# Forgetting attention with a channel mix on one core: the softmax division moved from the weights to the finished output

## The chip, the cores and the metric

The kernel runs on one core of a Trainium2 chip. Its time is device microseconds from the first to the last instruction of one execution; three runs of the kernel before took 919.32, 919.80 and 922.17 us, so 919.8 us is its median. A separate execution was taken by the hardware profiler, and everything said of instructions below comes from that one.

The core has five engines with a queue of instructions each: PE multiplies matrices, DVE, ACT and POOL work elementwise on vectors, and SP here issues every DMA. An engine takes its instructions strictly in the order in which the program lists them, so an instruction that waits also holds what stands behind it in its queue.

## The reference

```python
def _attn_ref(q, k, v, s):                    # 8 batches, 8 heads, 576 positions, head size 64
    scores = np.matmul(q, k.transpose(0, 1, 3, 2)) / np.sqrt(D)
    cum = np.cumsum(np.maximum(s, 0.0), axis=-1)
    bias = -(cum[:, :, :, None] - cum[:, :, None, :])
    scores = np.where(causal, -1e9, scores + np.minimum(bias, 0.0))
    attn = np.exp(scores - np.max(scores, axis=-1, keepdims=True))
    attn = attn / (np.sum(attn, axis=-1, keepdims=True) + 1e-09)
    return np.matmul(attn, v)

def _moe_ref(x, mu_k, mu_r, w_k, w_v, w_r):   # x: the 8 heads side by side, 512 wide; d_ff 1024
    x_prev = x shifted by one position, zero at the first
    xk = mu_k * x + (1.0 - mu_k) * x_prev
    xr = mu_r * x + (1.0 - mu_r) * x_prev
    k = np.maximum(xk @ w_k, 0.0)
    return 1.0 / (1.0 + np.exp(-(xr @ w_r))) * (k * k @ w_v)
```

The weights `w_k`, `w_v`, `w_r` arrive in double precision.

## The kernel before

**Attention, one head at a time.** A visit is one pair of heads of one batch. The 576 queries are cut into five tiles `t`: 64 queries first, then four times 128. Tile `t` sees keys 0 to `KN[t]` = 64, 192, 320, 448 or 576. Batch 0 is visited twice per pair, first with the tiles 0 to 2 (called A) and, when all four pairs are through, with the tiles 3 and 4 (called Z), so that the first rows of its output are ready early; the batches 1 to 7 are visited once per pair with all five tiles. That makes 4 + 4 + 28 = 36 visits and 72 heads' turns.

In `scores` a head's turn goes like this. PE multiplies queries by keys (L678; operands are split in a high and a low part, `KH` and `KL`, `G` holds both parts of q). DVE adds the bias `cb` or the masked bias `mask` and keeps the running minimum (L693), writing into the tile `W`. ACT takes the exponential of a whole row of tiles in place, with the row's sum in `sums` (L711). When all tiles of the head are through, POOL adds 1e-9 to the sums (L748), DVE takes the reciprocal `rinv` (L753), and POOL multiplies each tile of `W` by its row's reciprocal (L724): a query lies on a partition here, so the reciprocal is one scalar per partition. Rows 0 to 63 of tile 0 fill only 64 partitions.

`weighted` then turns `W` by PE transposes (L770; keys now lie on partitions), ACT and DVE split each turned block in a high part `ph` and a low part `pl` (L797, L801, L829, L836), PE multiplies by the values `V` (L903), and ACT and DVE add the two halves of the product into `xT` (L933, L937). `xT` holds the output of the pair transposed: partition 64 j + d is component d of head j, a column is a query. `finish` calls `weighted` for head j one head later than `scores`, and after the second head SP writes `xT` to the DRAM tensor `x_d` (L1231).

**Preparation.** POOL also makes the low parts of k, q and v (`KL` L607, `G` L618, `V` L563), the masks (L649) and the low parts of the weights (L538), which DVE and ACT first put together from the halves of the double precision words (L507 to L536).

**Channel mix.** 18 chunks of 256 positions. Each loads `x` from `x_d` (L1132), mixes it with its shifted self (ACT L979, DVE L988), splits the result (L1007, L1011), and then runs `hidden` (L1040), `gate` (L1082) and `output` (L1107) on PE. There is one buffer `x`, so the load for the next chunk waits until the last mix of the chunk before has read it.

**What sets the order.** All operations are first collected as tasks in a `Plan`. A task has an engine, an assumed duration, its dependencies and a due time, set by the program for each visit and chunk (`plan.due`). `Plan.forward` deals the tasks out engine by engine, earliest due time first among those that are ready, with assumed durations and assumed gaps between engines; `Plan.backward` derives new due times from the result; eight rounds are made, and the order of the best is emitted. So a change in a task's engine or length can move instructions everywhere in the program. While PE has nothing to do at the start, the plan fills it with multiplications of the identity (L359).

Of the kernel before, what the change touches and what calls it, by code (L numbers as in the profile page):

```python
# [285 lines left out]
def forgetting_attention_then_channel_mix(  # L286
# [19 lines left out]
    P = 128  # L306
# [18 lines left out]
    def sbuf(shape, tag, bufs=1, dtype=F32):  # L325
        return plan.buffer(sb, shape, dtype, tag, bufs)
# [4 lines left out]
    def fixed(t):  # L331
        b = Buffer(lambda: t)
        b.ap = t
        return b
# [13 lines left out]
    def pool(emit, reads, writes, n, extra, rate=0.8333):  # L348
        return plan.add("POOL", n * rate + extra, emit, reads, writes)

    def dma(emit, reads, writes, ns):
        return plan.add("SP", max(520, ns), emit, reads, writes, land=1300)
# [272 lines left out]
    def scores(b, h, tiles, G, KH, KL):  # L625
# [93 lines left out]
                [(nm, (t, mi))], [(W, i) for i in range(3)] + [(sums, t)], n, 280, 1,  # L719
            )  # L720

        def normalize(t, m, n, W):
            pool(
                lambda: nc.gpsimd.tensor_scalar(  # L724
                    out=W.ap[:m, :n],
                    in0=W.ap[:m, :n],
                    scalar1=rinv.get()[:m, t : t + 1],
                    scalar2=1.0,
                    op0=ALU.mult,
                    op1=ALU.mult,  # L730
                ),
                [rinv], [(W, i) for i in range(3)], n, 244,
            )

        def rs(x):
            return x.get()[:, tiles[0] : tiles[-1] + 1]

# [13 lines left out]
            [(sums, t) for t in tiles], [rinv], len(tiles), 100,  # L751
        )
        dve(lambda: nc.vector.reciprocal(rs(rinv), rs(rinv)), [], [rinv], 8 * len(tiles))  # L753
        for t in tiles:
            normalize(t, QN[t], KN[t], pt[t])
        return pt

    def weighted(j, pt, V, xT, tiles, plain):
# [194 lines left out]

    x_d = [fixed(dram.tile([P, NP, S + 1], F32, name=f"x_d{b}")) for b in range(B)]

    def channel_mix(ch, start, span):
# [263 lines left out]
    def finish(j, pt, V, xT, n, due):  # L1222
        b, hp, tiles = visits[n]
        plan.due = due
        weighted(j, pt, V, xT, tiles, n < PLAIN)
        if j == 1:
            q0, q1 = QS[tiles[0]], QS[tiles[-1]] + QN[tiles[-1]]

            c = slice(1 + q0 if q0 else 0, 1 + q1)
            dma(  # L1230
                lambda: nc.sync.dma_start(x_d[b].ap[:, hp, c], xT.get()[:, c]),  # L1231
                [(xT, 2)] + [(xT, (i, x)) for i in range(2) for x, _ in sums_of(tiles)],
                [(x_d[b], (hp, y)) for y in range(2) if tiles is ALL or y == (q0 > 0)],
                819,
            )
            if hp == NP - 1:
                there[b] = q1
# [69 lines left out]
```

## Time and profile before

| | us |
|---|---|
| median of three runs | 919.8 |
| span of the profiled execution | 919.5 |
| PE busy | 872.8 |
| DVE busy | 696.3 |
| ACT busy | 693.1 |
| POOL busy | 519.1 |
| of it, L724 (the division) | 165.2 |

The page gives busy time as a union over one engine; matrix multiplications overlap one another, so a PE that is always busy can still be short of its peak. The clock that PE was granted (1.00 is full speed) is given per stretch of time. "A <- B" in a table of waits means that A stood idle until B let it go. DMA issues are listed under SPq, the queue of SP; the time from issue to landing is given beside them.

### The profile page before, as it was taken

Reading aid. Unit: us, or ns where it says so; the run is one execution under the profiler, and the core shown is the slowest. Engines: PE = TensorE matmul, PEld = TensorE weight load, DVE = VectorE, ACT = ScalarE, POOL = GpSimd, SP = SyncE. Lnnn points to the kernel's source line nnn. Section 1 sums busy time; section 2 is a strip of 40 time slices with the busy share of each in tenths; the row PEclk is TensorE's granted clock in tenths of the full one; section 3 lists DMA queues with packets and bytes.
Section 4 is the critical chain, followed back from the end, with each engine's and each line's share of the span. In section 5 each row is a group of like instructions: output and inputs, shape, how many; then the busy total and the mean of one; then the engine's idle time right before and its main releaser. Section 6 shows DMA issues by size and latency. Waiting matters only on the chain. (4 is left out here: it accounts for less than half of the span.)

```text
span 919.5 us, 18649 instructions
## 1 busy us (share of the span) xinstructions
PE 872.8 (95%) x5546; PEld 758.6 (83%) x5546; DVE 696.3 (76%) x2473; ACT 693.1 (75%) x1834; POOL 519.1 (56%) x884
## 2 busy tenths in 40 slices
PE   6877879999999999999999999999999999998998
PEld 4656858987988898988889898989898979887886
DVE  6897998987987788778878778777787887546431
ACT  5888888998997898788968787878787876445331
POOL 6999599898576566556665646565556461100000
PEclk7568989999999999999999999999999999999999
DMA  6798645645344343434353525252434230101100
GB/s 195 223 257 237 206 123 160 174 142 168 100 151 129 109 152 87 145 112 144 100 151 93 163 61 159 79 152 79 147 97 138 79 89 25 42 31 35 46 24 23
DMA packets 65045, 110.89 MB, mean 121 GB/s; under 512 B 10544, under 2 KB 26416, under 8 KB 64944
## 3 DMA queue, kind: packets, MB, share of 16 engines
q1 hardware_dynamic: 64944, 109.71, 40.2%
q8 instruction: 43, 0.70, 0.3%
q14 instruction: 58, 0.48, 0.2%
HBM read 90.64 MB, written 19.04 MB: 119 GB/s over the span
## 5 line engine op out<-in xcount | busy, mean ns | idle before, releaser
L1040 PE MATMUL m<-xh,w_k 128*128 128x256 f32 x1152 | 231.4, 287 | 4.4 <-DVE kl L1069 4.4
L711 ACT ACTIVATE W<-W,nm 64x64 f32<-64x64 f32 (+4 forms) x320 | 179.7, 562 | 41.3 <-DVE nm L693 36.7
L770 PE MATMUL t<-ident,W 128*128 128x128 f32 (+1 forms) x960 | 188.3, 284 | 16.6 <-DVE ph L844 4.8
L1107 PE MATMUL m<-w_v,kh 128*128 128x512 f32 x576 | 198.4, 403 | 0.0
L1040 PEld LDWEIGHTS m<-xh,w_k 128*128 128x128 f32 x1152 | 186.2, 190 | 6.2 <-DVE kl L1069 4.8
L724 POOL TENSOR_SCALAR W<-W,rinv 64x64 f32<-64x64 f32 (+4 forms) x320 | 165.2, 538 | 10.6 <-DVE rinv L753 6.1
L1040 PE MATMUL m<-xl,w_k 128*128 128x256 f32 x576 | 164.6, 286 | 0.0
L770 PEld LDWEIGHTS t<-ident,W 128*128 128x128 f32 (+1 forms) x960 | 114.3, 133 | 47.5 <-DVE pl L801 7.9
L607 POOL TENSOR_TENSOR KL<-raw,KH 128x576 fp32r<-128x576 f32 (+1 forms) x72 | 98.5, 1370 | 79.8 <-ACT KH L603 73.4
L678 PE MATMUL s<-KH,G 128*128 128x288 f32 (+4 forms) x384 | 125.3, 335 | 11.3 <-ACT KH L603 5.3
L801 DVE TENSOR_TENSOR pl<-t,ph 128x256 fp32r<-128x256 f32 (+3 forms) x264 | 122.2, 472 | 16.0 <-ACT ph L797 14.7
L1107 PEld LDWEIGHTS m<-w_v,kh 128*128 128x128 f32 x576 | 106.2, 189 | 18.2 <-DVE r L530 0.2
L678 PE MATMUL s<-KL,G 128*128 128x288 f32 (+4 forms) x384 | 118.5, 312 | 2.4 <-POOL KL L607 2.4
L797 ACT CAST ph<-t 128x256 fp32r<-128x256 f32 (+3 forms) x264 | 107.3, 414 | 13.0 <-PE t L770 11.5
L1107 PE MATMUL m<-w_v,kl 128*128 128x512 f32 x288 | 117.0, 406 | 0.0
L693 DVE CUSTOM_DVE_ANT_0 W<-s,cb 128x320 f32<-128x320 f32 (+3 forms) x256 | 94.9, 375 | 26.4 <-PE s L678 21.7
L903 PE MATMUL po<-ph,V 128*128 128x448 f32 (+4 forms) x344 | 109.6, 326 | 3.7 <-ACT ph L797 1.8
L1040 PEld LDWEIGHTS m<-xl,w_k 128*128 128x128 f32 x576 | 109.2, 190 | 0.9
L618 POOL TENSOR_TENSOR G<-raw,G 64x576 fp32r<-64x576 f32 (+2 forms) x72 | 93.6, 1300 | 27.4 <-issue 13.2
L988 DVE SCALAR_TENSOR_TENSOR xp<-x,mu,xp 128x256 f32<-128x256 f32 (+3 forms) x192 | 80.4, 419 | 37.2 <-ACT xp L979 33.9
L979 ACT ACTIVATE xp<-x,mu 128x256 f32<-128x256 f32 (+3 forms) x192 | 81.5, 424 | 29.3 <-DVE xl L1011 9.7
L1082 PE MATMUL m<-w_r,xh 128*128 128x512 f32 x288 | 101.9, 407 | 0.0
(97 smaller groups left out, 1751.7 us busy)
## 6 DMA issues: line engine op xcount, KB each, us to landing
raw<-in_k SPq DMA_DIRECT2D x128, 144.0 KB, 3.2
cb<-cum_d SPq DMA_DIRECT2D x64, 288.0 KB, 3.6
raw<-in_q SPq DMA_DIRECT2D x112, 144.0 KB, 3.3
vn<-in_v SPq DMA_DIRECT2D x32, 320.0 KB, 3.8
out<-g SPq DMA_DIRECT2D x36, 256.0 KB, 2.1
x_d<-xT SPq DMA_DIRECT2D x28, 288.5 KB, 2.3
x<-x_d SPq DMA_DIRECT2D x12, 514.0 KB, 4.0
w_k<-in_moe_w_k SPq DMA_DIRECT2D x8, 512.0 KB, 5.3
```

Of the source, the lines that this page charges most:

```text
L607: lambda k=k, kh=kh, kl=kl: nc.gpsimd.tensor_tensor(out=kl.get(), in0=k.get(), in1=f32(kh.get()), op=ALU.subtract),
L678: lambda x=x, K=K: nc.tensor.matmul(ps.get()[:m, :w], G.get()[:, q0 : q0 + m], K.get()[:, k0 : k0 + w], start=x == 0, stop=x == 1,),
L693: lambda a=a, e=e, bias=bias, i=i: nc.vector.tensor_tensor_reduce(out=W.ap[:m, a:e], in0=ps.get()[:m, a - k0 : e - k0], in1=bias.get()[:m, ...
L711: lambda: nc.scalar.activation(W.ap[:m, :n], W.ap[:m, :n], AF.Exp, bias=nm.get()[:m, 3 * t + mi : 3 * t + mi + 1], scale=-1.0, accum_out=s ...
L724: lambda: nc.gpsimd.tensor_scalar(out=W.ap[:m, :n], in0=W.ap[:m, :n], scalar1=rinv.get()[:m, t : t + 1], scalar2=1.0, op0=ALU.mult, op1=AL ...
L770: lambda: nc.tensor.transpose(ps.get()[0:m, place : place + P], pt[t].ap[:, k0 : k0 + m], ident.ap),
L797: act(lambda: nc.scalar.copy(strips(ph), src()), [ps], [(ph, k) for k in ks], n * m)
L801: lambda: nc.vector.tensor_tensor(out=strips(pl), in0=src(), in1=f32(strips(ph)), op=ALU.subtract),
L903: lambda: nc.tensor.matmul(po.get()[: P if both else 64, at + q0 - base : at + q0 - base + m], V.get()[:, kb, 2 * j : 2 * j + (2 if both e ...
L1040: lambda u=u, f=f, c=c, n=n, w=w, x=x: nc.tensor.matmul(ps.get()[:, u * CT : (u + 1) * CT], weight["k", c, f // 4].get()[:, w, f % 4 * P : ...
L1082: lambda c=c, n=n, x=x, w=w: nc.tensor.matmul(ps.get(), x.get()[:, c, ts], weight["r", c, 0].get()[:, w], start=c == 0 and n == 0, stop=c ...
L1107: lambda f=f, n=n, x=x, w=w: nc.tensor.matmul(ps.get(), x.get()[:, f, ts], weight["v", f, 0].get()[:, w], start=f == 0 and n == 0, stop=f ...
```

## The change

The tiles `W` stay as the exponentials leave them. `normalize` is removed. Instead, each head's reciprocals go by DMA to a new DRAM tensor `rinv_d` of the batch, laid out by head and query: tile 0 (64 partitions, one column) in one DMA, the other tiles (128 partitions, one column each) in a second, so that each element of 4 bytes lands on its own. When the second head of a pair is finished, two DMAs read the rows of both heads back, each broadcast to 64 partitions, into a new tile `R` with two buffers, so that `R` has the layout of `xT`. POOL multiplies the finished `xT` by `R` once, and only then SP writes `xT` to `x_d`. The last line of the diff shrinks a reserve of on-chip memory that belongs to DMAs issued by POOL, of which the kernel has none.

```diff
-        def normalize(t, m, n, W):
-            pool(
-                lambda: nc.gpsimd.tensor_scalar(
-                    out=W.ap[:m, :n],
-                    in0=W.ap[:m, :n],
-                    scalar1=rinv.get()[:m, t : t + 1],
-                    scalar2=1.0,
-                    op0=ALU.mult,
-                    op1=ALU.mult,
-                ),
-                [rinv], [(W, i) for i in range(3)], n, 244,
-            )
-
 ...
         dve(lambda: nc.vector.reciprocal(rs(rinv), rs(rinv)), [], [rinv], 8 * len(tiles))
-        for t in tiles:
-            normalize(t, QN[t], KN[t], pt[t])
+        for ts in ((0,), tuple(t for t in tiles if t)):
+            if ts[0] in tiles:
+                q0, m, n = QS[ts[0]], QN[ts[0]], len(ts)
+                dma(
+                    lambda ts=ts, q0=q0, m=m, n=n: nc.sync.dma_start(
+                        rinv_d[b].ap[h, q0 : q0 + n * m].rearrange("(t p) -> p t", p=m),
+                        rinv.get()[:m, ts[0] : ts[-1] + 1],
+                    ),
+                    [rinv], [(rinv_d[b], (h, t)) for t in ts], 100 * n,
+                )
         return pt
 ...
+    rinv_d = [fixed(dram.tile([H, S], F32, name=f"rinv_d{b}")) for b in range(B)]
     x_d = [fixed(dram.tile([P, NP, S + 1], F32, name=f"x_d{b}")) for b in range(B)]
 ...
         if j == 1:
             q0, q1 = QS[tiles[0]], QS[tiles[-1]] + QN[tiles[-1]]
 
+            R = sbuf([P, q1 - q0], "R", 2)
+            for i in range(2):
+                dma(
+                    lambda i=i: nc.sync.dma_start(
+                        R.get()[64 * i : 64 * i + 64],
+                        rinv_d[b].ap[2 * hp + i : 2 * hp + i + 1, q0:q1].broadcast_to([64, q1 - q0]),
+                    ),
+                    [(rinv_d[b], (2 * hp + i, t)) for t in tiles], [(R, i)], 410 * (q1 - q0) / S,
+                )
+            parts = [(xT, (i, x)) for i in range(2) for x, _ in sums_of(tiles)]
+            pool(
+                lambda: nc.gpsimd.tensor_tensor(
+                    out=xT.get()[:, 1 + q0 : 1 + q1],
+                    in0=xT.get()[:, 1 + q0 : 1 + q1],
+                    in1=R.get(),
+                    op=ALU.mult,
+                ),
+                [(R, 0), (R, 1)], parts, q1 - q0, 114, 2.21,
+            )
             c = slice(1 + q0 if q0 else 0, 1 + q1)
             dma(
                 lambda: nc.sync.dma_start(x_d[b].ap[:, hp, c], xT.get()[:, c]),
 ...
-    nc = bacc.Bacc("TRN2", target_bir_lowering=False, num_devices=1)
+    nc = bacc.Bacc("TRN2", target_bir_lowering=False, num_devices=1, dynamic_dma_scratch_size=1024)
```

The numbers 100, 410, 114 and 2.21 are what the plan assumes of the new tasks; they set its order, not their true length.

**How the order moves.** The first pairs of batch 0 on POOL. `rinv_293` and `rinv_338` are the reciprocals of the two heads of the first pair, `W_0_...` and `W_1_...` their weight tiles; `KL`, `G`, `V` and `mask` are prepared for heads to come. Before:

```order
L724 TENSOR_SCALAR W_0_72<-W_0_72,rinv_293 128x192
L724 TENSOR_SCALAR W_0_73<-W_0_73,rinv_293 128x320
L748 TENSOR_SCALAR rinv_338<-sums_115 128x3
L607 TENSOR_TENSOR KL_340<-raw_101,KH_312 128x320
L607 TENSOR_TENSOR KL_219<-raw_106,KH_214 128x320
L724 TENSOR_SCALAR W_1_76<-W_1_76,rinv_338 64x64
L649 AFFINE_SELECT mask_183<-cb_155 64x64
L724 TENSOR_SCALAR W_1_77<-W_1_77,rinv_338 128x192
L649 AFFINE_SELECT mask_183<-cb_155 128x256
L724 TENSOR_SCALAR W_1_78<-W_1_78,rinv_338 128x320
```

After, the same place (line numbers are the changed kernel's):

```order
L618 TENSOR_TENSOR G_189<-raw_109,G_189 64x320
L563 TENSOR_TENSOR V_312<-vn_161,V_312 128x3x64
L607 TENSOR_TENSOR KL_336<-raw_111,KH_326 128x320
L735 TENSOR_SCALAR rinv_347<-sums_120 128x3
L563 TENSOR_TENSOR V_312<-vn_161,V_312 128x3x64
L607 TENSOR_TENSOR KL_251<-raw_114,KH_230 128x320
L618 TENSOR_TENSOR G_217<-raw_149,G_217 64x320
L637 MEMSET sums_120 128x1
L538 TENSOR_TENSOR w_k_00_362<-xh_215,w_k_00_362 128x512
L607 TENSOR_TENSOR KL_261<-raw_111,KH_244 128x320
```

The divisions are gone and the preparation of the next pairs follows directly on the reciprocal.

SP's queue up to the first write of `x_d`. `raw` are k and q on their way to be split, `cb` the bias rows, `w_k` a block of the weights. Before:

```order
L630 DMA cb_168<-cum_d 128x320
L588 DMA raw_101<-in_k 64x320 x2
L588 DMA raw_103<-in_q 64x320
L588 DMA raw_106<-in_k 64x320 x2
L588 DMA raw_103<-in_q 64x320
L484 DMA w_k_10_526<-in_moe_w_k 128x1024
L630 DMA cb_155<-cum_d 128x320
L1231 DMA x_d_89<-xT_110 128x321
```

After:

```order
L1228 DMA R_445<-rinv_d_89 64x320
L630 DMA cb_178<-cum_d 128x320
L1228 DMA R_445<-rinv_d_89 64x320
L484 DMA w_k_10_460<-in_moe_w_k 128x1024
L588 DMA raw_114<-in_k 64x320
L588 DMA raw_109<-in_q 64x320
L745 DMA rinv_d_89<-rinv_307 64x1
L745 DMA rinv_d_89<-rinv_307 128x2x1
L588 DMA raw_109<-in_q 64x320
L630 DMA cb_178<-cum_d 128x320
L588 DMA raw_114<-in_k 64x320
L1246 DMA x_d_97<-xT_134 128x321
```

Two reads of `R` and two writes of reciprocals now stand between the loads of k, q and `cb`; the write of a head's reciprocals comes several rows ahead of the read of the same values.

SP's queue at the end of the attention: the last two pairs, and the load of `x` for the third chunk from the end, whose first columns come from batch 6 and whose last 65 wait for the last pair of batch 7. Before:

```order
L1231 DMA x_d_96<-xT_110 128x577
L1132 DMA x_918<-x_d_95 128x4x193
L1124 DMA out<-g_1306 128x512
L1124 DMA out<-g_1375 128x512
L1231 DMA x_d_96<-xT_128 128x577
L1132 DMA x_918<-x_d_96 128x4x65
```

After:

```order
L1228 DMA R_539<-rinv_d_96 64x576
L1246 DMA x_d_104<-xT_134 128x577
L745 DMA rinv_d_96<-rinv_347 64x1
L745 DMA rinv_d_96<-rinv_347 128x4x1
L1128 DMA x_895<-x_d_103 128x4x193
L1228 DMA R_539<-rinv_d_96 64x576
L1120 DMA out<-g_1291 128x512
L1120 DMA out<-g_1357 128x512
L1246 DMA x_d_104<-xT_138 128x577
L1128 DMA x_895<-x_d_104 128x4x65
```

Both halves of the last `R` are read ahead of two writes of `out`, so before the last `x_d`; the last `x_d` now waits for POOL's product instead of DVE's sum.

## The prediction, made before the change was run

> **What bounds the kernel now.** I read the stretches first, since the share of busy time over the whole span mixes three very different parts.
>
> ```profile
> core 0: us, PE busy (x) PEld busy (x) DVE busy (x) ACT busy (x) POOL busy (x), PEclk, DMA share, GB/s
> 0.00:20.00 20.00, 12.01 (x61) 8.56 (x62) 11.20 (x32) 10.61 (x25) 13.07 (x38) 0.80 0.71 196
> 20.00:67.00 47.00, 37.95 (x161) 27.35 (x160) 43.26 (x161) 38.43 (x121) 43.44 (x86) 0.61 0.80 236
> 67.00:92.00 25.00, 19.29 (x111) 15.35 (x110) 19.98 (x62) 20.91 (x51) 23.53 (x31) 0.80 0.86 237
> 92.00:141.00 49.00, 39.76 (x232) 33.21 (x232) 47.16 (x158) 42.11 (x104) 38.00 (x55) 0.90 0.52 164
> 184.00:736.00 552.00, 544.99 (x3625) 482.66 (x3625) 439.88 (x1659) 455.12 (x1229) 342.07 (x579) 1.00 0.41 122
> 812.00:842.00 30.00, 27.51 (x167) 24.19 (x165) 14.80 (x30) 13.36 (x29) 0.00 (x0) 1.00 0.15 50
> ```
>
> From 184 to 736 us PE is busy 544.99 of 552.00 us at full clock: there PE is the bound, and an engine that becomes less busy beside it earns almost nothing. After 812 us POOL is empty. What a lighter POOL can earn lies in batch 0, from 20 to 92 us: POOL is busy 43.44 of 47.00 and 23.53 of 25.00 us, 93% of 72 us. But DVE is at 43.26 of 47.00 beside it, and from 92 to 141 us DVE is the fullest engine with 47.16 of 49.00 us, or 96.2%. The DMAs are at 0.80 and 0.86. PE is not the bound there.
>
> Next, who waited for the division, and for what PE waits from 20 to 67 us:
>
> ```profile
> engine op xcount: duration ns min/median/max, first and last start us, forms
> ...
>   PEld t L770: 6.7, 13
>   PE t L770: 3.0, 6
> ```
> ```profile
> PEld po L903 <- ACT ph L797: 4.7, 8, 1.1
> PEld t L770 <- DVE pl L836: 4.2, 7, 1.5
> ...
> PEld t L770 <- POOL W L724: 3.2, 6, 1.0
> ...
> PE t L770 <- POOL W L724: 1.4, 3, 0.8
> ```
>
> The first two rows are the waiters on L724 over the whole span: PE lost 3.0 us in 6 waits, its weight loads 6.7 us. In the front ACT and DVE hold up PE's loads at least as long (4.7 and 4.2 us) as POOL's division does (3.2 us).
>
> **What is removed.** POOL's 320 divisions, by stretch:
>
> ```profile
> 20.00:67.00 47.00, 11.26 (x26) 0.61 0.80 236
> 67.00:141.00 74.00, 12.20 (x19) 0.86 0.64 189
> 141.00:812.00 671.00, 141.74 (x275) 1.00 0.39 117
> sum 792.00, POOL 165.20; mean POOL 55.07
> ```
> ```profile
> 67.00:92.00 25.00, 4.12 (x6) 0.80 0.86 237
> ```
> ```profile
> L724 POOL TENSOR_SCALAR W<-W,rinv 64x64 f32<-64x64 f32 (+4 forms) x26 | 11.3, 445 | 0.1
> ```
>
> From 20 to 92 us that is 11.26 + 4.12 = 15.4 us of POOL's 67.0. The last row is the group from 20 to 67 us: only 0.1 us of idle time stood before its 26 instructions, so POOL was never waiting for them to become ready; they were late because POOL was full.
>
> **What POOL gets instead.** 36 products of two inputs on `xT`. The trace has the same operation and shape as KL and, for the 256 columns of a Z visit, as G:
>
> ```profile
> L607 POOL TENSOR_TENSOR KL<-raw,KH 128x576 fp32r<-128x576 f32 x64 | 91.7, 1433 | 79.5 <-ACT KH L603 73.4 <-DMA w_v<-in_moe_w_v 4.8
> L607 POOL TENSOR_TENSOR KL<-raw,KH 128x320 fp32r<-128x320 f32 x8 | 6.8, 867 | 0.3
> L618 POOL TENSOR_TENSOR G<-raw,G 64x256 fp32r<-64x256 f32 x8 | 5.9, 734 | 0.7
> ```
>
> 28 x 1.433 + 4 x 0.867 + 4 x 0.734 = 46.5 us, so POOL falls by 118.7 to about 400 us. In 20 to 92 us come the four A pairs and one Z pair, 3.5 + 0.7 = 4.2 us: POOL goes from 67.0 to 55.8 of 72 us, 78%, and is no longer the bound.
>
> **The front term.** DVE keeps all its work. Its 43.26 + 19.98 = 63.2 us at the 96.2% that it reaches from 92 to 141 us would take 65.7 us instead of 72.0: at most 6.3 us can be had. The other bound is 0, if ACT (59.3 of 72 us) and the DMAs hold the stretch where it is. Of the three waits of PE's loads shown above POOL's division is 3.2 of 12.1 us, yet POOL also holds up q and k; between the two ends I take the middle, -3.1 us.
>
> **The middle term.** Of PE's 3.0 us of waits 1.4 lie before 67 us; 1.6 are left, and half of it will be a wait for the exponential instead: -0.8 (0 to -1.6). The 141.74 us of division after 141 us lie beside a full PE and earn nothing more.
>
> **DMAs added.** Writes: two per head in A (16) and in batches 1 to 7 (112), one in Z (8), 136; reads of R: 2 x 36 = 72. All go through SP.
>
> ```profile
> L588 SPq DMA_DIRECT2D raw<-in_q x16: 466/546/767, 19.8 to 63.4; - x16
> L588 SPq DMA_DIRECT2D raw<-in_k x16: 465/544/596, 24.9 to 62.1; - x16
> ...
> DMA to landing us min/median/max: 2.2/4.5/6.6
> ```
> ```profile
> SPq L630 <- DVE nm L693: 7.1, 5, 1.9
> SPq L1231 <- DVE xT L937: 2.9, 2, 2.3
> ```
> ```profile
> mu<-in_moe_mu_k SPq DMA_DIRECT2D x1, 2.0 KB, 1.8
> mu<-in_moe_mu_r SPq DMA_DIRECT2D x1, 2.0 KB, 3.1
> ...
> x_d<-xT SPq DMA_DIRECT2D x28, 288.5 KB, 2.3
> raw<-in_k SPq DMA_DIRECT2D x128, 144.0 KB, 3.2
> ```
>
> An issue takes SP 0.33 us when the queue is quiet (the last x_d below) and 0.55 us in a run; 208 of them are 69 to 114 us of SP over the whole span, hidden, since nothing but DMAs is in that queue and the middle has few. In 20 to 67 us the 32 loads of q and k alone take 32 x 0.545 = 17.4 us of SP, and SP already stands waiting (10 us in its two largest waits). The 16 writes and 8 reads of the A visits put 8 to 13 us more there. I cost them at nothing, because the order puts each read several rows behind the write that it needs and the loads run ahead of their use; if that cover is gone, rival 1 has the price. What queues behind a write that waits for its reciprocal are loads of q, k and cb, and for these wait KL, G and the masks on POOL. On POOL, V, KL and a mask stand behind a product that waits for R.
>
> A read of R moves 144 KB to 64 partitions, as a load of k does, landing after 3.2 us; all of R is 9.2 MB. A write moves 64 or up to 512 single elements of 4 bytes, 64 x 576 = 36,864 in all. For their cost there is no row; the nearest are the two loads of mu, 128 rows of 16 bytes, which land after 1.8 and 3.1 us, like any other transfer. From above, a packet could cost as much as a mean one:
>
> ```profile
> DMA packets 65045, 110.89 MB, mean 121 GB/s; under 512 B 10544, under 2 KB 26416, under 8 KB 64944
> q1 hardware_dynamic: 64944, 109.71, 40.2%
> ```
>
> 919.5 x 16 x 0.402 / 64,944 = 91 ns. The 8 x 320 elements of A would then take 2560 x 91 / 16 = 14.6 us of each DMA engine, and with 47 x 0.80 + 25 x 0.86 = 59.1 us already there the front would be full at 73.7 of 72 us, before R. From below it is near nothing, as the rows of mu have it; I take that end, and leave the other to the range.
>
> The page "DMA: Bandwidth & Descriptors" of the Trainium skill, sections "Specifications" and "Bandwidth", speaks against the change at this point: transfers below 512 B are read, modified and written back, and its table has a floor of about 10.5 ns a packet. By that floor the estimate is 36,864 x 10.5 / 16 = 24 us of each engine over the whole span, hidden; by the read-modify-write it could be more, and no row here shows which.
>
> **The end.** The last pair's chain grows by the product.
>
> ```profile
> 811.91 0.63 DVE L937 TENSOR_TENSOR xT<-po,xT 64x448 f32<-64x448 f32 x1
> 812.61 0.33 SPq L1231 DMA_DIRECT2D x_d<-xT  x1
> 814.78 0.53 SPq L1132 DMA_DIRECT2D x<-x_d  x1
> ```
> ```profile
> 825.65 0.69 DVE L1011 TENSOR_TENSOR xl<-xp,xh 128x512 fp32r<-128x512 f32 x1 [0.65 <-ACT xh L1007]
> ```
> ```profile
> 827.78 0.28 PE L1040 MATMUL m<-xh,w_k 128*128 128x256 f32 x1
> ```
>
> SP starts the write 0.07 us after DVE's sum has ended. With 1.43 us of product and a second handing over it is 1.55 us later, and so is x. Cover: PE has the gate and output of the chunk before until 827.78 us, and the low part that it needs next is ready at 826.34, so 1.44 us are hidden. R itself is read long before. The rest is 0.1; some of the elementwise work behind it slides too, so +0.5 (0 to +1.6, with no cover).
>
> **Sum.** 919.5 - 3.1 - 0.8 + 0.5 = 916.1 us of span. The median of the runs is 0.3 us above the profiled execution, so 916.4.
>
> **The rivals.**
>
> 1. *SP becomes the bound of the front: slower.* From 20 to 67 us the added issues fall on a queue that works 28 of 47 us (the timeline has 56 issues of about 0.5 us there, 32 of them the q and k rows above). Where an added issue meets a moment in which SP works, everything behind it is late. At the quiet 0.33 to the busy 0.55 us, 24 issues are 7.9 to 13.2 us; 28 / 47 of that is 4.7 to 7.9, say 6: 919.8 + 6 = 925.8. It decides when POOL and DVE wait for loads more than the 3.1 us that the division gives back. For it: in-order SP, waits already there, 4.5 us of landing. Against: POOL was the full engine, and its rows in the front wait for almost no DMA.
> 2. *No change.* DVE, ACT and the DMAs hold the front at its length, a wait for POOL turns into a wait for DVE's pl; only the end pays: 919.8 + 0.5 = 920.3. For it: DVE 43.26 beside POOL 43.44. Against: DVE's 5 us of idle time in 67 to 92 us, where POOL alone is full.
> 3. *The front packs much better.* PE runs there at a clock of 0.61, 0.80 and 0.90, against 1.00 later, since it stands still so often. With fewer stalls the clock comes up, each head's chain through PE shortens, and DVE loses all its idle time of 20 to 141 us, 3.74 + 5.02 + 1.84 = 10.6 us: 919.8 - 10.6 = 909.2. The page "TensorE: Matmul & The Clock Gate", Part 1, has such a rule: half the clock after an idle window of about 3.4 us, all of it after a busy one. The low clock of these rows agrees. Against: DVE has never been seen above 96.2%.
>
> That the sums no longer reach the result is excluded: the product takes the place of the division, and nothing else in the weights' path depends on their scale.
>
> **How the numbers follow.** Forecast 0.46, rival 1 0.20, rival 2 0.20, rival 3 0.14. The forecast's own terms run from -6.3 - 1.6 + 0 to 0 + 0 + 1.6. The range takes in half of rival 3's side and rival 1: 908.5 to 925.5 us. About 0.3%, 2.8 us, is what can be told from no change here: faster means below 917.0, slower above 922.6. The forecast lies mostly under the first (0.33 of its 0.46), with rival 3 that is 0.47; no change is rival 2 and 0.10 of the forecast, 0.30; slower is rival 1 and the rest, 0.23.
>
> **What would show it.** Right: POOL from 20 to 92 us at about 78% and DVE above 92%; the first load of x earlier than before by some 3 us; the stretch with PE at 98.7% unchanged in length; the last x_d 1.5 us after DVE's sum. Wrong: SP rows with waits on rinv and landings of R in the front, followed by POOL or ACT waiting for raw; writes of rinv_d that land far later than 2.3 us; a product on POOL with idle time before it on a DMA, and PE waiting for the next KL.

## The result and the profile after

The change takes 1194.2 us in the median (four runs, 1183.3 to 1195.5) beside 919.6 us for the kernel before on the same chip: a ratio of 1.295 (95% interval 1.290 to 1.301), 29.5% slower. The forecast was 916.4 us, the range ended at 925.5. An execution more than 1.5% above the fastest of its kernel is left out of the medians below. The profiled execution has a span of 1181.5 us. Its page, in part:

```profile
span 1181.5 us, 18619 instructions
...
PE 935.6 (79%) x5540; PEld 799.3 (68%) x5540; DVE 704.8 (60%) x2473; ACT 695.7 (59%) x1834; POOL 400.1 (34%) x600
...
DMA packets 109845, 120.49 MB, mean 102 GB/s; under 512 B 50736, under 2 KB 67632, under 8 KB 109744
...
q1 hardware_dynamic: 109744, 119.31, 57.9%
...
DMA 38%; PE 29%; ACT 10%; issue 9%; DVE 8%; POOL 4%; SPq 2%; POOLq 0%; ACTq 0%; DVEq 0%
DMA rinv_d<-rinv 13%; PE m L1036 10%; DMA x<-x_d 8%; PE m L1103 6%; DMA raw<-in_k 5%; PE m L1078 4%; DMA raw<-in_q 4%; PE t L765 3%; DMA cb<-cum_d 3%; PE s L678 3%; PE po L898 3%; ACT xp L975 2%; ACT W L711 2%; DVE xp L984 2%; DVE W L693 2%
```

POOL is at the 400 us that the sum had for it, so the division is gone and the product costs what its rows said. The chain that ended last (the last two rows, shares of the span) runs through DMAs for 38%, 13% through the writes of the reciprocals alone. The table of stretches shows that the loss is nowhere in particular:

```profile
20.00:67.00 47.00, 22.15 (x96) 15.60 (x95) 22.38 (x95) 22.68 (x75) 24.46 (x45) 0.60 0.76 121
67.00:92.00 25.00, 13.82 (x51) 9.66 (x50) 14.62 (x52) 11.79 (x38) 9.00 (x14) 0.57 0.70 108
92.00:141.00 49.00, 31.04 (x149) 25.67 (x148) 32.14 (x93) 29.49 (x68) 24.42 (x32) 0.67 1.00 185
184.00:736.00 552.00, 441.45 (x2691) 380.25 (x2692) 342.12 (x1298) 349.64 (x948) 209.77 (x301) 0.90 0.65 108
```

From 20 to 67 us PE gets through 96 multiplications where it had 161. From 184 to 736 us, where it had been busy 98.7%, it does 2691 in place of 3625. In that stretch the DMA engines are busier (0.65 against 0.41) and move less (108 against 122 GB/s). A part of the loss comes back at PE, which stands still more often: its granted clock is 0.90 there in place of 1.00 (the last column but two), and over the whole span a multiplication of the channel mix (L1036, L1040 before) takes 298 ns in the mean in place of 287. Who waits for the transfers stands in the waits of SP's queue, and in those of the other engines (us in total, times, longest us):

```profile
SPq L1228 <- DMA rinv_d<-rinv: 421.8, 69, 10.0
```
```profile
POOL mask L649 <- DMA cb<-cum_d: 157.4, 48, 9.9
...
ACT xp L975 <- DMA x<-x_d: 111.2, 22, 13.1
```

Before, POOL's masks and ACT's mixing waited for the same two loads almost never:

```profile
ACT xp L979 <- DMA x<-x_d: 7.1, 5, 3.4
...
POOL mask L649 <- DMA cb<-cum_d: 2.6, 3, 1.0
```

SP, which issues every transfer in order, stands 421.8 us in 69 waits, 6.1 us each, for writes of `rinv_d` to land, before it can issue the read of R (L1228). One such wait in the timeline of SP, with the two writes before it and the load of `cb` behind it:

```profile
502.76 1.32 SPq L745 DMA_DIRECT2D rinv_d<-rinv  x2
513.35 0.45 SPq L1228 DMA_DIRECT2D R<-rinv_d  x1
513.89 0.85 SPq L630 DMA_DIRECT2D cb<-cum_d  x1
```
```profile
517.75 0.82 POOL L649 TENSOR_SCALAR_AFFINE_SELECT mask<-cb 64x64 f32<-64x64 f32 x2 [7.32 <-DMA cb<-cum_d]
```

The second row of SP starts 9.3 us after the writes have been issued; `cb` behind it is late, and POOL has stood idle for 7.32 us when its mask can begin. In the table of stretches for the time between, the DMA share is the last column but one:

```profile
502.00:504.00 2.00, 1.04 (x6) 0.56 (x5) 2.00 (x9) 0.85 (x2) 0.83 (x3) 1.00 0.90 288
504.00:506.00 2.00, 2.00 (x14) 1.56 (x14) 2.00 (x10) 1.64 (x6) 0.10 (x1) 1.00 0.33 61
506.00:513.00 7.00, 7.00 (x38) 5.75 (x38) 4.55 (x19) 6.25 (x16) 1.76 (x3) 1.00 0.00 0
```

For 7 us no packet is recorded on any of the 16 engines, and SP goes on only after that. The written elements themselves had been quick. From 504.5 to 505.0 us the trace has

```profile
DMA packets 499, 0.02 MB, mean 36 GB/s; under 512 B 492, under 2 KB 492, under 8 KB 499
q1 hardware_dynamic: 499, 0.02, 57.3%
```

which is 0.5 us x 16 x 0.573 / 499 = 9.2 ns a packet. Most of the 576 elements of the two writes are through by then, over 8 us before SP may go on.

### The profile page after: what moved, and what is told of

Read it like the earlier page. It is cut to its first block, busy times and chain, and to the rows that moved or that the text cites. A ratio compares the mean times of both kernels' runs of the same rounds, so it can differ in the third digit from the quotient of the medians.

```text
span 1181.5 us, 18619 instructions
## 1 busy us (share of the span) xinstructions
PE 935.6 (79%) x5540; PEld 799.3 (68%) x5540; DVE 704.8 (60%) x2473; ACT 695.7 (59%) x1834; POOL 400.1 (34%) x600
## 4 chain that ended last, share of the span: by engine, by line
DMA 38%; PE 29%; ACT 10%; issue 9%; DVE 8%; POOL 4%; SPq 2%; POOLq 0%; ACTq 0%; DVEq 0%
DMA rinv_d<-rinv 13%; PE m L1036 10%; DMA x<-x_d 8%; PE m L1103 6%; DMA raw<-in_k 5%; PE m L1078 4%; DMA raw<-in_q 4%; PE t L765 3%; DMA cb<-cum_d 3%; PE s L678 3%; PE po L898 3%; ACT xp L975 2%; ACT W L711 2%; DVE xp L984 2%; DVE W L693 2%
## 5 line engine op out<-in xcount | busy, mean ns | idle before, releaser
L765 PE MATMUL t<-ident,W 128*128 128x128 f32 (+1 forms) x960 | 209.8, 300 | 95.2 <-DVE pl L796 43.6
L1036 PE MATMUL m<-xh,w_k 128*128 128x256 f32 x1152 | 244.8, 298 | 16.9 <-DVE kl L1065 14.8
L765 PEld LDWEIGHTS t<-ident,W 128*128 128x128 f32 (+1 forms) x960 | 120.7, 139 | 133.4 <-DVE pl L796 56.7
L1036 PEld LDWEIGHTS m<-xh,w_k 128*128 128x128 f32 x1152 | 196.9, 200 | 20.6 <-DVE kl L1065 15.9
L1103 PE MATMUL m<-w_v,kh 128*128 128x512 f32 x576 | 208.2, 418 | 0.1
L678 PE MATMUL s<-KH,G 128*128 128x288 f32 (+4 forms) x384 | 132.4, 355 | 86.1 <-DVE nm L693 78.1
L1036 PE MATMUL m<-xl,w_k 128*128 128x256 f32 x576 | 170.2, 296 | 0.4 <-DVE xl L1007 0.4
L678 PEld LDWEIGHTS s<-KH,G 128*128 128x128 f32 (+1 forms) x384 | 77.5, 203 | 106.5 <-DVE nm L693 90.3
L898 PE MATMUL po<-ph,V 128*128 128x448 f32 (+4 forms) x344 | 118.3, 352 | 30.3 <-ACT ph L792 28.3
L649 POOL TENSOR_SCALAR_AFFINE_SELECT mask<-cb 128x512 f32<-128x512 f32 (+2 forms) x136 | 54.2, 417 | 185.8 <-DMA cb<-cum_d 157.4
L1036 PEld LDWEIGHTS m<-xl,w_k 128*128 128x128 f32 x576 | 115.3, 200 | 1.7 <-DVE xl L1007 0.8
```

Of the source, the lines that this page charges most:

```text
L678: lambda x=x, K=K: nc.tensor.matmul(ps.get()[:m, :w], G.get()[:, q0 : q0 + m], K.get()[:, k0 : k0 + w], start=x == 0, stop=x == 1,),
L765: lambda: nc.tensor.transpose(ps.get()[0:m, place : place + P], pt[t].ap[:, k0 : k0 + m], ident.ap),
L898: lambda: nc.tensor.matmul(po.get()[: P if both else 64, at + q0 - base : at + q0 - base + m], V.get()[:, kb, 2 * j : 2 * j + (2 if both e ...
L1036: lambda u=u, f=f, c=c, n=n, w=w, x=x: nc.tensor.matmul(ps.get()[:, u * CT : (u + 1) * CT], weight["k", c, f // 4].get()[:, w, f % 4 * P : ...
L1103: lambda f=f, n=n, x=x, w=w: nc.tensor.matmul(ps.get(), x.get()[:, f, ts], weight["v", f, 0].get()[:, w], start=f == 0 and n == 0, stop=f ...
```

## The experiments

Three things come into question: the 136 writes of single elements, SP standing in order behind them, and what else came with the change (reads, products, a new order). Theory W says that the writes cost everything, its rival V that the rest does. Within W, W1 puts the cost on SP's standing, W2 on the writes slowing every other transfer.

### The change without its writes

```diff
-        for ts in ((0,), tuple(t for t in tiles if t)):      # the two writes of rinv_d per head
-            ...
-                        rinv_d[b].ap[2 * hp + i : 2 * hp + i + 1, q0:q1].broadcast_to([64, q1 - q0]),
+                        cum_d.ap[b * H + 2 * hp + i : b * H + 2 * hp + i + 1, q0:q1].broadcast_to([64, q1 - q0]),
...
```

> The changed kernel without the 136 writes of reciprocals; R is read from rows of cum_d, so the output is scaled by wrong numbers, while every other instruction of the change is there (72 reads of R, 36 products, no divisions). Theory W, the single-element writes and what waits for them cost everything: 913 to 920 us, near the forecast of 916.4, since that is all of the change but the writes. Theory V, the reads of R, the products or the plan's new order cost it: above 1000 us.

Measured: 926.1 us, ratio 1.0065 (1.0046 to 1.0085). Without the writes 268 us are gone: reads and products, all in place, do not cost the time. But it is no gain either, +0.65%, outside of what W expected; the last two experiments take that up.

### The writes, and nobody waits for them

All 136 writes stay; R is read from `cum_d` as in the kernel above.

```diff
-                        rinv_d[b].ap[2 * hp + i : 2 * hp + i + 1, q0:q1].broadcast_to([64, q1 - q0]),
+                        cum_d.ap[b * H + 2 * hp + i : b * H + 2 * hp + i + 1, q0:q1].broadcast_to([64, q1 - q0]),
...
```

> The changed kernel with all 136 single-element writes, but R is read from rows of cum_d, so no read waits for a write to land (the output is scaled by wrong numbers). Theory W1, SP stands still at the read of R until the write has landed (421.8 us in 69 waits in the changed kernel) and the loads behind it come late: 915 to 930 us. Theory W2, the writes slow every other transfer, whether anyone waits for them or not: above 1050 us.

Measured: 1116.6 us, ratio 1.2141 (1.2098 to 1.2184), in the median of three executions; the profiled one, from which the rows below are, took 1131.6. So 190.5 of the 268.1 us come from writes that nobody waits for. The other 77.6 come with the reads that wait for them. SP's standing is what the trace shows for these; that the reads also fetch elements just written, which this kernel leaves out too, was not tried by itself. The waits of the other engines say how the writes cost time unread:

```profile
POOL mask L649 <- DMA cb<-cum_d: 129.0, 42, 8.8
...
ACT xp L975 <- DMA x<-x_d: 83.6, 21, 7.3
```
```profile
184.00:736.00 552.00, 460.53 (x2850) 400.34 (x2851) 357.59 (x1371) 371.18 (x1003) 215.29 (x314) 0.93 0.75 112
```

The loads of `cb` and `x` are late here too, although no read of R waits for the writes: the DMA engines are at 0.75 in place of 0.41 and move 112 GB/s. The writes slow the transfers beside them.

### Larger pieces, and pieces further apart

If it is the single elements, then their number, size and place must count. The first kernel lays a head's queries out so that the columns of a partition lie side by side: pieces of 16 bytes (8 in the visits A and Z, 4 in tile 0), 13,312 in place of 36,864, again end to end.

```diff
-                        rinv_d[b].ap[h, q0 : q0 + n * m].rearrange("(t p) -> p t", p=m),
+                        rinv_d[b].ap[h, q0 : q0 + n * m].rearrange("(p t) -> p t", p=m),
```

> The changed kernel with each partition's reciprocals written side by side, 16 bytes (8 in A and Z) at a time: 64 + 128 pieces per head instead of 576, the reads of R wait as before; the order of the elements in DRAM is wrong, so the output is too. If the landing time goes with the number of pieces, 10 us of the longest wait becomes about 2 + 8 x 192 / 576 = 4.7 us and the kernel takes 960 to 1040 us. If it is a fixed price of any write of less than a row, it stays above 1150 us.

The second keeps the 36,864 single elements and sets them 64 bytes apart. Its tensor is filled first by eight copies, one per batch, so that R, read from a stretch of it, is defined; the read waits for the write as before.

```diff
-                        rinv_d[b].ap[h, q0 : q0 + n * m].rearrange("(t p) -> p t", p=m),
+                        rinv_d[b].ap[h, q0 : q0 + n * m, 0:1].rearrange("(t p) o -> p (t o)", p=m),
...
-    rinv_d = [fixed(dram.tile([H, S], F32, name=f"rinv_d{b}")) for b in range(B)]
+    rinv_d = [fixed(dram.tile([H, S, 16], F32, name=f"rinv_d{b}")) for b in range(B)]
...
+    def fill(b):
+        dma(
+            lambda: nc.sync.dma_start(
+                rinv_d[b].ap.rearrange("h q x -> h (q x)"),
+                k[b, :, 0:16, :].rearrange("h d s -> h (d s)"),
+            ),
...
```

> The changed kernel with the same 576 single elements per head, but each 64 bytes from the next in DRAM instead of 4; the reads of R wait for the same writes and read a filled stretch of the same tensor (wrong numbers; 8 copies of 288 KB fill it, added work of some us at the start). If the price is one per piece wherever it lands: 1150 to 1250 us. If the pieces are slow because neighbours fall into the same stretch of DRAM and wait for each other: below 1000 us.

Measured: 1015.3 us (ratio 1.1037, 1.0995 to 1.1079) for the larger pieces, and 928.9 us (1.0097, 1.0074 to 1.0121) for the same single elements 64 bytes apart. The same number of packets of the same size costs next to nothing once they don't lie side by side. The spaced kernel reads R from other places than it has just written, but that is not what makes it cheap: the kernel with unread writes, which reads none of the elements it writes, has 190.5 us of the price all the same. SP's wait for the writes, in the larger pieces and then in the spaced elements, and the landing of the spaced writes (the last number, median us from issue):

```profile
SPq L1228 <- DMA rinv_d<-rinv: 242.4, 63, 6.5
```
```profile
SPq L1228 <- DMA rinv_d<-rinv: 48.4, 34, 2.9
```
```profile
rinv_d<-rinv SPq DMA_DIRECT2D x56, 2.0 KB, 2.6
```

Three more distances, with 8, 4 and 2 floats in place of 16:

> The change with the single elements 32 bytes apart in place of 4 (64 bytes took 929 us). R is read from a filled stretch, so the numbers are not the reference's. If neighbours disturb each other only within 32 bytes: 925 to 935, SP's waits for rinv_d some 50 us. If they do within 64 bytes, two elements then share one such piece in place of sixteen: 940 to 1000. If the cost goes by the bytes that a write spans: between 64 bytes and 4, but near the first, 930 to 945.

> The change with the single elements 16 bytes apart; R is read from a filled stretch, so the numbers are not the reference's. 64 bytes apart took 929 us, 32 bytes 932, 4 bytes 1194. If what disturbs is a neighbour within 32 bytes (two elements now share it): 945 to 1000. If it is within 64 bytes, 32 bytes apart would already have shown it, so that is no longer expected. If only touching elements disturb each other: 925 to 938. If the cost falls smoothly with the distance: 940 to 960.

> The change with the single elements 8 bytes apart; R is read from a filled stretch, so the numbers are not the reference's. If a piece of 32 bytes is the unit (four elements share it): 980 to 1100. If only touching elements disturb each other: 925 to 940. If the cost falls smoothly with the distance: 960 to 1050.

And two controls: the dense writes of the change with the filling, since filling had come in together with the distance, and the 16-byte pieces with a gap of their own size behind each (`rearrange("(p t) x -> p (t x)", p=m)[:, 0:n]` in a tensor of two floats per query).

> The change with its single elements end to end as they were (4 bytes apart), but its DRAM tensor filled by 8 copies of 18 KB first, as in the spaced kernels; the output is still the full computation. If the distance is what counts: 1180 to 1200, as the change. If it was the filling that made the spaced kernels cheap: below 1000.

> The 13,312 pieces of the kernel with 16-byte pieces, each now with a gap of as many bytes behind it (32 bytes from start to start; 8 bytes for the 4-byte ones); R is read from a filled stretch, so the numbers are not the reference's. End to end they took 1015 us, 89 us above the kernel without writes. If pieces that touch set the price: 930 to 945. If every small piece has it, touching or not, or if it goes by the bytes written into the neighbourhood: 1000 to 1020.

The rows of the DMA queue (packets, MB, share of 16 engines' span) of the kernel without writes and of the one with 64 bytes' distance:

```profile
q1 hardware_dynamic: 70704, 119.15, 44.0%
```
```profile
q1 hardware_dynamic: 109872, 121.67, 46.8%
```

The share times the span is the time that each engine had packets under way: 924.9 x 0.440 = 407.0 us without writes, 926.5 x 0.468 = 433.6 us with the spaced ones, and 1181.5 x 0.579 = 684.1 us in the change. On which packets the time lies can be read from the trace's packet records, each with its duration and its size. Of the 277 us that the change adds per engine, 26.7 lie on packets of up to 16 bytes, among them the written elements, and 249.5 on packets of over 512 bytes, although these are 59,008 in both kernels. Their median stays at 93 ns, but 1619 of them take over 1 us, where 37 did without writes. So the small packets don't hold the engines; they make packets of other transfers late. In the spaced kernel the small packets add 20.2 us, and 6.1 us lie on large ones, the filling among them.

The last two columns of the table are the mean durations of the packets of each kind; without writes they are 10.0 and 108 ns. The time above 926.1 us, the kernel without writes, is that of the medians.

| piece, bytes | start to start, bytes | pieces | median, us | ratio (95%) | above 926.1 us | packets up to 16 B, ns | packets over 512 B, ns |
|---|---|---|---|---|---|---|---|
| 4 (the change) | 4 | 36,864 | 1194.2 | 1.295 (1.290 to 1.301) | 268.1 | 10.7 | 176 |
| 4, filled | 4 | 36,864 | 1165.1 | 1.265 (1.259 to 1.271) | 239.0 | 9.6 | 171 |
| 4 | 8 | 36,864 | 980.0 | 1.065 (1.063 to 1.067) | 53.9 | 9.1 | 133 |
| 4 | 16 | 36,864 | 947.7 | 1.030 (1.027 to 1.032) | 21.6 | 8.7 | 120 |
| 4 | 32 | 36,864 | 932.3 | 1.013 (1.011 to 1.015) | 6.2 | 8.7 | 111 |
| 4 | 64 | 36,864 | 928.9 | 1.010 (1.007 to 1.012) | 2.8 | 8.6 | 110 |
| up to 16 | end to end | 13,312 | 1015.3 | 1.104 (1.100 to 1.108) | 89.2 | 9.9 | 136 |
| up to 16 | twice the piece | 13,312 | 956.4 | 1.039 (1.036 to 1.042) | 30.3 | 9.1 | 122 |

The filling is not it: filled and dense it still takes 1165 us (why 29 us less than the change, I did not find out). Pieces end to end cost nearly the same in both kernels, 268.1 us / 36,864 = 7.3 ns and 89.2 / 13,312 = 6.7 ns of the kernel's time each, although 7,168 of the 13,312 have 16 bytes and 2,048 have 8; the other 4,096 are single elements here too. A gap as large as the piece takes away two thirds (larger pieces) or four fifths (4 bytes) of it, and each further doubling more than half of the rest; at 32 and 64 bytes it can't be told from what another order of the work does, below. The price falls steadily, so none of the thresholds that I had named (pieces of 32 or 64 bytes that neighbours share, or touching alone) explains all rows. Why neighbours in DRAM make the transfers beside them late, and what happens between the last packet and the landing, stays open.

### The reciprocals turned first

What the change wants can be had without small pieces: PE turns the reciprocals of a head, and each write is one to four rows of 256 or 512 bytes.

```diff
+        pe(
+            lambda: nc.tensor.transpose(ps.get()[0:nt, 0:P], rs(rinv), ident.ap),
+            [rinv, ident], [ps], P, nt, 2 / 2.4,
+        )
+        act(lambda: nc.scalar.copy(rT.get()[0:nt], ps.get()[0:nt, 0:P]), [ps], [rT], P, 150)
...
-                        rinv_d[b].ap[h, q0 : q0 + n * m].rearrange("(t p) -> p t", p=m),
-                        rinv.get()[:m, ts[0] : ts[-1] + 1],
+                        rinv_d[b].ap[h, q0 : q0 + n * m].rearrange("(t p) -> t p", p=m),
+                        rT.get()[i : i + n, 0:m],
```

> The full computation of the change, with one thing other: PE turns the reciprocal sums by a transpose, ACT copies them out, and each write is one to four rows of 256 or 512 bytes that lie in one piece in DRAM, in place of 64 to 512 single elements. The reads of R wait for these writes as in the change. Theory N (single elements at neighbouring addresses cost the time): no slow pieces are left, so it falls from 1194 to near the kernel without writes, 926 us, and somewhat above it for one more transpose on PE per head (64 x some 0.1 us): 924 to 934, and SP's waits for rinv_d below 40 us (the spaced elements had 48.4). Rival R (it is the way through DRAM, a write and a read that waits for it, that costs): above 960, SP's waits above 150 us. Should the -3.9 us that were forecast for the division exist, it is below 919.

Measured: 937.6 us, ratio 1.0187 (1.0172 to 1.0202). The way through DRAM, with its write and its waiting read, is now within 11.5 us of the kernel without writes, and SP's waits for it are small. The first two rows are of this kernel, the third is PE's row of the kernel without writes:

```profile
PE 887.1 (95%) x5611; PEld 763.2 (82%) x5611; DVE 704.9 (75%) x2473; ACT 705.5 (75%) x1906; POOL 400.1 (43%) x600
```
```profile
SPq L1237 <- DMA rinv_d<-rT: 32.4, 28, 2.0
```
```profile
PE 873.5 (94%) x5536; PEld 756.5 (82%) x5536; DVE 702.1 (76%) x2473; ACT 694.0 (75%) x1834; POOL 400.2 (43%) x600
```

It misses the expected 924 to 934 by 4 us: PE is busy 13.6 us longer, 0.19 us for each of the 72 added transposes, not the 0.1 I had put down, on the engine that bounds the middle. That this is all of the 11.5 us is likely but not shown, since the order is another one too.

### The division taken away, and nothing in its place

The kernel of the change without writes, reads and products; the output stays unscaled.

> The division is taken away, and neither writes, reads nor products are put in its place: the output is left unscaled. It leaves POOL 165 us lighter, which is the term of the forecast alone. Forecast (POOL is the bound of the front): 919.7 - 3.1 - 0.8 = 915.8, not above 917. Rival 2 (DVE, ACT and the DMAs hold the front): 919 to 921, the front's first part early by some 7 us as in the kernel without writes and given back by the second chunk at 225 us. If the kernel without writes lost its 6.5 us to the reads and products alone, this one is 6 us or more below it; if to the order that the planner makes of a lighter POOL, it stays near 925.

Measured: 918.9 us, ratio 0.9988 (0.9977 to 1.0000). A POOL lighter by 165 us, with the order that the planner then makes, gains 1.6 us of span (917.9 against 919.5), where the forecast had 3.9. What the lighter POOL is worth by itself is not settled by that, since an order alone is worth more, as the next kernels show.

### Other orders of the same instructions

The kernel without writes adds 72 reads and 36 products to the one just shown and lies 7.2 us above it. To see what the planner's order alone can do, one assumed number is changed: the extra time of a division in the kernel before, 144 and 344 ns in place of 244, and that of the product in the kernel without writes, 14 in place of 114. The instructions stay the same.

```diff
-                [rinv], [(W, i) for i in range(3)], n, 244,
+                [rinv], [(W, i) for i in range(3)], n, 144,
```

> The kernel before, with one number of the planner changed: the extra time that it assumes for a division on POOL is 144 ns in place of 244. The instructions are the same, only their order moves, and with it nothing that the change is about. If the order by itself is harmless: 917 to 922.5, within 0.3% of the kernel before. If the planner's order alone is worth some 6 us, as the +6.5 us of the kernel without writes may be: outside of that, most likely 923 to 928.

> The kernel before with the planner's extra time for a division at 344 ns in place of 244 (144 ns took 927 us). Same instructions, other order. If the order before lies at a low point and every other order nearby loses some us: 922.5 to 930. If a longer assumed division orders the work at least as well: 916 to 922.5.

> The kernel without writes (926 us, R read from a table that lies in DRAM from the start, so the numbers are not the reference's), with one number of the planner changed: the extra time assumed for the product is 14 ns in place of 114. The instructions are the same. If that kernel's +6.5 us over the kernel before are the work of its reads and products: 924 to 928 again. If they are the order's, this order is another draw: anything from 917 to 930, and outside of 924 to 928 rather than in it.

Measured: 927.2 us with 144 (ratio 1.0073, 1.0059 to 1.0087), 928.7 with 344 (1.0082, 1.0060 to 1.0103), and 922.1 for the kernel without writes in another order (1.0017, 1.0002 to 1.0032), against 926.1. So an order that differs in nothing but one planner's number is worth 4 to 8 us, as much as the whole +6.5 of the kernel without writes; that these 6.5 are the order's alone is not shown. The number 244 lies between two that are both slower. The stretches show where it goes. Multiplications of PE are counted in parentheses, the fillers with the identity (L359) among them; before, no division, no writes, and before with 144:

```profile
0.00:141.00 141.00, 109.02 (x562) 84.47 (x562) 121.60 (x411) 112.05 (x296) 118.05 (x207) 0.77 0.70 206
141.00:276.00 135.00, 132.43 (x888) 116.11 (x887) 117.59 (x478) 123.99 (x348) 108.19 (x180) 1.00 0.50 149
276.00:736.00 460.00, 455.17 (x3037) 405.07 (x3037) 361.28 (x1343) 371.03 (x995) 272.31 (x461) 1.00 0.40 119
```
```profile
0.00:141.00 141.00, 110.71 (x590) 88.33 (x591) 123.86 (x421) 115.20 (x306) 102.42 (x172) 0.81 0.73 213
141.00:276.00 135.00, 132.78 (x877) 116.07 (x876) 119.28 (x483) 125.55 (x350) 69.12 (x106) 0.99 0.50 148
276.00:736.00 460.00, 452.30 (x3032) 400.74 (x3031) 360.50 (x1337) 368.04 (x987) 176.43 (x272) 1.00 0.39 117
```
```profile
0.00:141.00 141.00, 110.92 (x568) 86.06 (x568) 123.83 (x412) 112.28 (x297) 104.83 (x173) 0.79 0.77 223
141.00:276.00 135.00, 130.91 (x873) 113.55 (x872) 118.64 (x480) 125.77 (x346) 76.59 (x113) 1.00 0.55 159
276.00:736.00 460.00, 451.58 (x3019) 399.99 (x3018) 361.56 (x1333) 366.18 (x984) 202.65 (x294) 1.00 0.44 129
```
```profile
0.00:141.00 141.00, 116.59 (x568) 90.50 (x569) 122.00 (x412) 111.18 (x294) 119.88 (x208) 0.73 0.70 206
141.00:276.00 135.00, 131.51 (x873) 114.05 (x872) 116.63 (x476) 124.21 (x348) 105.17 (x178) 0.99 0.50 147
276.00:736.00 460.00, 453.83 (x3018) 401.31 (x3017) 360.20 (x1333) 366.35 (x984) 268.17 (x453) 1.00 0.41 119
```

The fillers do no work and have to be left out of the count; they all lie before 141 us. In the same order of kernels they are:

```profile
0.00:141.00 141.00, 12.24 (x58) 6.96 (x58) 0.77 0.70 206
```
```profile
0.00:141.00 141.00, 9.55 (x49) 5.95 (x49) 0.81 0.73 213
```
```profile
0.00:141.00 141.00, 10.07 (x48) 6.43 (x48) 0.79 0.77 223
```
```profile
0.00:141.00 141.00, 11.83 (x52) 6.66 (x52) 0.73 0.70 206
```

A multiplication takes 460 / 3037 = 0.15 us in the middle. Without division PE is 590 - 49 - (562 - 58) = 37 of them ahead at 141 us, 26 at 276 and 21 at 736 us, or 3.2 us, of which the span keeps 1.6. The front does gain, and nearly half of that is given back by 736 us. The kernel without writes, 16 ahead at 141 us, is 17 behind at 736 (2.6 us of its 5.4 in span); before with 144 goes much the same way, from 12 ahead to 22 behind, with no change in its work. The loss of the middle is a PE with a few more gaps, 451.58 to 453.83 of 460 us where the kernel before has 455.17.

## Why the prediction was wrong

**The step that failed** is the price of the writes: "For their cost there is no row; the nearest are the two loads of mu, 128 rows of 16 bytes ... From below it is near nothing, as the rows of mu have it; I take that end". In its place come 268.1 us, 190.5 of them through slower transfers and 77.6 more when the reads wait for the writes. Two things went wrong in it. The rows of mu are loads, each of 128 pieces into 128 partitions; what costs here is a small piece written beside others of the same write, and no row of before shows that. And the sum asked only what the packets of the writes cost themselves, and took their landing for that of any other transfer. The packets do cost little: 9.2 ns each in the half microsecond above. But SP stands up to 10.0 us for a landing, where the loads of mu had 1.8 and 3.1, and there was no term for what the writes do to the rest, 249.5 us of each engine in packets of other transfers. The upper bound of 91 ns, a mean packet of the kernel before, had it no better. That 36,864 x 91 / 16 = 210 us would have come near the 268.1 is chance, for the written elements don't take 91 ns. The bound was also left out of the range, against what the prediction says: the 14.6 us that it gives for the front are not in it, and the range's end of 925.5 even lies just below rival 1's own 925.8.

The Trainium skill, page "DMA: Bandwidth & Descriptors", sections "Specifications" and "Bandwidth", had been weighed at this point. Its floor of about 10.5 ns a packet, given there for loads that GpSimd issues, is near the durations of the small packets here, 8.6 ns in the mean with 64 bytes' distance and 10.7 end to end; but these do not hold the price. Its warning, that transfers below 512 B are read, modified and written back, pointed the right way; but the elements 64 bytes apart are as small as the others and cost nearly nothing, so by these runs it is not the size alone.

**"I cost them at nothing, because the order puts each read several rows behind the write that it needs."** The order does not give that cover: 15 of the 72 reads in the changed kernel follow a write of `rinv_d` with no row between, 42 with at most two, and in the last pair shown under "How the order moves" it is one. Where the writes land soon that is nearly enough: with turned reciprocals, 45 of 72 reads as close, SP waits 32.4 us in all. For landings that keep it standing up to 10.0 us it is not. What the prediction said would be queued behind, loads of k, q and `cb`, and the masks on POOL, is just what waits.

**Rival 1**, SP as the bound, has the right engine and a wrong mechanism: issues cost little (the turned kernel has all 208 of them), and SP stands for landings, over the whole span and not in the front.

**The front term**, -3.1 (0 to -6.3), and **the middle term**, -0.8: with the division taken away together -1.6 us. By 276 us PE was 26 multiplications ahead, 3.9 us, so the front's size was about right; but the middle, put at a small gain, took 0.8 us back by 736 us. With 4 to 8 us between one order and another, even that much agreement may be luck. POOL from 20 to 92 us was forecast at 55.8 us busy, and DVE as the next bound. POOL has 36.68 + 18.81 = 55.5 us in the kernel without writes:

```profile
20.00:67.00 47.00, 34.40 (x143) 25.78 (x143) 40.94 (x152) 38.84 (x119) 36.68 (x63) 0.62 0.83 244
67.00:92.00 25.00, 20.61 (x122) 17.90 (x123) 22.25 (x69) 21.20 (x51) 18.81 (x25) 0.83 0.78 242
```

DVE has 63.2 us there, as before. Without division, and nothing in its place, it is DVE that is nearest to full, with 66.41 of 72.00 us, or 92%:

```profile
20.00:92.00 72.00, 56.30 (x292) 45.15 (x291) 66.41 (x239) 62.97 (x179) 53.73 (x86) 0.75 0.84 246
```

Of the rivals, the second, no change, is what the division alone gives by the 0.3% bound, and the third, a front that gains 10 us, is not borne out at the end.

**The end.** The product was forecast at 1.43 us, and the write of `x_d` 1.5 us after DVE's sum:

```profile
1071.22 0.63 DVE L932 TENSOR_TENSOR xT<-po,xT 64x448 f32<-64x448 f32 x1
1071.93 1.43 POOL L1236 TENSOR_TENSOR xT<-xT,R 128x576 f32<-128x576 f32 x1 [29.37 <-DVE xT L932]
1073.39 0.33 SPq L1246 DMA_DIRECT2D x_d<-xT  x1
```

DVE's sum ends at 1071.22 + 0.63 = 1071.85, and the write starts 1.54 us later. **What the prediction did not have at all** is the order: a planner that lays out the instructions anew for any change moves this kernel by 4 to 8 us, more than the forecast's whole gain, so that even without the writes the sign was open.

## What to carry to other kernels

Before a layout is turned by a DMA, count its pieces and ask whether they lie end to end in DRAM: with rows of 256 or 512 bytes this kernel took 937.6 us, with single floats side by side 1194.2. The recorded time of the small packets does not give the price, since it falls on other transfers and on the landing; one such write with a wait behind it, in a trace, shows it. A landing on which an in-order queue waits is paid by everything behind it, so such a price comes twice, in the transfers and in the queue. And where a planner orders the work, run the old kernel once with a slightly other order before a gain below 1% is believed or forecast.

## What the runs showed of the hardware

- The records of the 4-byte writes are as short end to end as 64 bytes apart: all packets of up to 16 bytes took 10.7 and 8.6 ns in the mean, 9 in the median in both. What differs is the packets of over 512 bytes beside them: 176 and 110 ns in the mean, 93 in the median in both, with 1619 and 85 of some 59,000 over 1 us.
- Between the last recorded packet of one such write and the end of SP's wait for it lay 7 us in which the engines recorded nothing at all (DMA share 0.00 from 506 to 513 us). Whether the memory is still busy with them can't be seen in the trace.
- Other transfers are slowed with nobody waiting for the writes: 0.75 of the engines' time for 112 GB/s from 184 to 736 us, where 0.41 had moved 122.
